# Whole-block normalisation and transposes, an even stride for the value rows, and a gate/up opening on 256 rows, in a fused attention and gated-MLP kernel

## The chip, the cores and the metric

The kernel runs on one core of one Trainium2 chip. The metric is device time in microseconds (us) from launch to end, the median of several executions. The profile of one execution gives a span 1.8 to 2.0 us shorter than the time measured for it. Where two kernels are compared, the numbers come from the same session on the same chip unless the text says otherwise.

## The reference, cut to what matters

```python
xn = layernorm(x)                                   # x: 2048 x 512, bf16
q  = (xn @ wq) -> 32 heads x 2048 x 128
p  = softmax(q @ k_cache^T * 128**-0.5)             # 2048 keys a head
s  = (p @ v_cache) -> 2048 x 4096, then @ wo        # 2048 x 512
g  = silu((relu(xn @ W_gate) * (xn @ W_up)) @ W_down)   # F = 1792
out = x + s * g
```

## The kernel before

The program first computes the gated MLP (160 us), then attention in 128 blocks. A block is one head and 512 query rows. It has 16 key tiles of 128 keys, taken in pairs. TensorE does, for each tile, one score matmul (512 columns) and four value matmuls (one for each 128 query rows, 129 columns: 128 values and a column of constants that sums the softmax denominator). ScalarE takes the exponential of a pair. The blocks are also the place where the query projection of the next head and the output projection of the last group of four heads (16 blocks) are done, one piece at the start of each block.

The value tile has rows of 129 elements, so 258 bytes:

```python
VW = Dh + 1                                          # 129
V_sb = [S_([128, KT, VW], BF16, "V_sb") for _ in range(2)]
...
def emit_PV_tile(gp, tt):
    ...
    for j in range(4):
        bank = j // 2
        if t == 0 and j % 2 == 0:
            _wait(pe, norm_tok[b - 1][bank] if b >= 1 else acc_free[bank])
        o_ap = ps_acc[:, bank, (j % 2) * 256:(j % 2) * 256 + VW]
        ins = pe.matmul(o_ap, PT[pb][:, tt, j * 128:(j + 1) * 128], V_sb[vb][:, t, :], ...)
```

At the end of a block, each of the two PSUM banks with its output is normalised by itself, and each 128 x 128 piece is transposed by its own DMA. The buffers for the normalised output number 16, one group, so VectorE waits at the first block of a group until every transpose of the group before has landed:

```python
NON = G * QB                                         # 16 buffers
def emit_norm_bank(b, bank, pvtok):
    _wait(dve, pvtok)
    if bank == 0 and b % (G * QB) == 0 and g >= 1:
        _wait(dve, t_tok(g - 1))
    rztok = dve.reciprocal(rz_sb[:, bank, :, :], z_ap)          # 128 x 2
    for jj in range(2):
        tok = dve.tensor_scalar(Onorm[ob][:, j, :], ps_acc[:, bank, base:base + Dh],
                                rz_sb[:, bank, jj, :], None, op0=ALU.mult)   # 128 x 128
    ...
    for jj in range(2):
        sp.dma_start_transpose(OT_store[...128 columns...], Onorm[ob][:, j, :])
```

The head of the program: 12 dummy matmuls to raise TensorE's clock, layer norm of the first four row tiles (two on GpSimd, two on VectorE), their transposes, and then gate and up on 512 rows for each 128 columns of the weights (`...` marks cuts):

```python
FCS = [0, min(2, FC), min(8, FC), FC]                # weights arrive in three parts
load_w(sp, Wg_sb, wg_src, sem_wg, 0)
load_w(act, Wu_sb, wu_src, sem_wu, 0)
...
for _i in range(12):
    pe.matmul(ps_acc[:, 0, 0:D], warm[:, 0:128], warm[:], start=True, stop=True)
head_ln()             # transposes of row tiles 0 to 3, then gate/up from the first column block on
```

The softmax here doesn't subtract the row's maximum and nothing guards it: scores larger than these inputs give would overflow.

Of the kernel before, what the change touches and what calls it, by code (L numbers as in the profile page):

```python
# [5 lines left out]
BF16 = mybir.dt.bfloat16  # L6
# [45 lines left out]
def bass_recurrent_scan__mha_block_cached__glu_gated_reglu__prompt_kernel(  # L52
# [33 lines left out]
    NON = G * QB  # L86
# [4 lines left out]
    TPG = 16 * 4 * G * QB  # L91
# [12 lines left out]
    with ExitStack() as es:  # L104
# [23 lines left out]
        V_sb = [S_([128, KT, VW], BF16, "V_sb") for _ in range(2)]  # L128
# [68 lines left out]
        with nc.Block() as block:  # L197

            @block.tensor
            def _(_pe_eng):  # L200
# [13 lines left out]
                FCS = [0, min(2, FC), min(8, FC), FC]  # L214
# [24 lines left out]
                load_w(act, Wu_sb, wu_src, sem_wu, 0)  # L239
# [103 lines left out]
                def head_transpose(n, ntok, eng, sem):  # L343
                    tp_ps = ps_r[:, n, :].bitcast(BF16)
# [13 lines left out]
                    ring_tok[n // 2].append(ctok)  # L358

                def head_ln():  # L360
                    st = ln_stats(0)
                    st = ln_stats(1)
                    sq01 = ln_aggr([0, 1], st)
                    st = ln_stats(2)
                    c01 = ln_coef([0, 1], sq01)
                    n0 = ln_norm(pool, sem_nm, 0, c01)
                    n1 = ln_norm(pool, sem_nm, 1, c01)
                    st = ln_stats(3)
                    sq23 = ln_aggr([2, 3], st)
                    c23 = ln_coef([2, 3], sq23)  # L370
                    n2 = ln_norm(dve, sem_ln4, 2, c23)
                    n3 = ln_norm(dve, sem_ln4, 3, c23)
                    head_transpose(0, n0, act, sem_xa)
                    head_transpose(1, n1, act, sem_xa)
                    head_transpose(2, n2, act, sem_xa)
                    head_transpose(3, n3, dve, sem_xt)

# [27 lines left out]

                def emit_gate_up(Q):
                    qs = slice(Q * NQ, (Q + 1) * NQ)
                    par = Q % 2
                    h_tok = None
                    for fc in range(FC):  # L410
                        fs = slice(fc * 128, (fc + 1) * 128)
                        s = ring_acquire()
# [16 lines left out]
                        gk = fc % NSLOT  # L429
                        _wait(act, gtok)  # L430
                        _wait(act, gr_free[gk])
                        rtok = sem_relu.sig(act.activation(gr_sb[gk][:], ps_r[:, gb, :], ACTF.Relu))  # L432
                        _wait(dve, gu_tok)
                        _wait(dve, rtok)
                        if fc == 0:
                            _wait(dve, hT_free[par])
                        h_tok = sem_h.sig(
                            dve.tensor_tensor(hT[par][:, fc, :], gr_sb[gk][:], ps_r[:, gb + 1, :], ALU.mult)  # L438
                        )
                        gr_free[gk] = h_tok  # L440
                        ring_tok[s] = [rtok, h_tok]
                        if Q == 0:
                            ln_task(fc)
# [33 lines left out]
                for _i in range(12):  # L477
                    pe.matmul(ps_acc[:, 0, 0:D], warm[:, 0:128], warm[:], start=True, stop=True)
                head_ln()
                ring_cnt[0] = 2  # L480
# [7 lines left out]
                rz_sb = S_([128, 2, 2, 1], F32, "rz_sb")  # L488
# [108 lines left out]
                def emit_norm_bank(b, bank, pvtok):  # L597
# [4 lines left out]
                    if bank == 0 and b % (G * QB) == 0 and g >= 1:  # L602
                        _wait(dve, t_tok(g - 1))
                    z_ap = ps_acc[:, bank, :].rearrange("p (j w) -> p j w", j=2)[:, :, Dh:Dh + 1]
                    rztok = sem_rz.sig(dve.reciprocal(rz_sb[:, bank, :, :], z_ap))  # L605
                    _wait(dve, rztok)
                    tok = None
                    for jj in range(2):
                        j = 2 * bank + jj
                        base = jj * 256  # L610
                        tok = sem_norm.sig(
                            dve.tensor_scalar(  # L612
                                Onorm[ob][:, j, :], ps_acc[:, bank, base:base + Dh],
                                rz_sb[:, bank, jj, :], None, op0=ALU.mult,
                            )
                        )
                    if b == NBLK - 1:
                        emit_last_transposes(hh, Q, ob, bank, tok)
                        return tok
                    _wait(sp, tok)  # L620
                    if bank == 0 and b % (G * QB) == 0 and g >= 2:
                        _wait(sp, opg_tok.get(g - 2))
                    tsem = sem_t[g % 2] if g < NG - 1 else sem_tl[Q]
                    for jj in range(2):
                        j = 2 * bank + jj
                        tsem.sig(
                            sp.dma_start_transpose(  # L627
                                OT_store[g % 2][:, hh, Q * NQ + j * 128:Q * NQ + (j + 1) * 128],
                                Onorm[ob][:, j, :],
                            )  # L630
                        )
# [26 lines left out]
                def emit_PV_tile(gp, tt):  # L658
# [11 lines left out]
                    for j in range(4):  # L670
# [4 lines left out]
                        ins = pe.matmul(o_ap, PT[pb][:, tt, j * 128:(j + 1) * 128], V_sb[vb][:, t, :],  # L675
                                        start=(t == 0 and j % 2 == 0), stop=(t == KT - 1 and j % 2 == 1))
                        if t == KT - 1 and j == 1:
# [3 lines left out]
                    if t == KT - 1:  # L681
# [3 lines left out]
                        ntx = emit_norm_bank(b, 0, tx)  # L685
                        nty = emit_norm_bank(b, 1, ty)
                        norm_tok[b] = (ntx, nty)
# [126 lines left out]
```

## Time and profile before

| | before |
|---|---|
| time, median of the first 3 runs | 1299.66 us (1298.06 to 1300.32) |
| span of the profile (of an execution that took 1300.44 us) | 1298.6 us |
| first value matmul starts at | 160.5 us |
| block period, blocks 1 to 15 / later | 8.254 / 8.835 us |
| gaps of TensorE after the first value matmul | 8.3 us |

The head of the page: busy time, share of the span, instructions. In all views PE is TensorE's matmuls, PEld its weight loads, DVE VectorE, ACT ScalarE, POOL GpSimd, and SPq the queue from which SyncE issues DMAs; L675 is line 675 of the kernel.

```profile
span 1298.6 us, 27683 instructions
...
PE 1287.6 (99%) x11968; PEld 835.3 (64%) x11968; DVE 442.5 (34%) x1190; ACT 1001.6 (77%) x1109; POOL 11.5 (1%) x23
...
## 4 chain that ended last, share of the span: by engine, by line
PE 93%; DVE 3%; SPq 2%; DMA 1%; issue 0%; ACT 0%; DVEq 0%
```

"PE 99% busy" says little, since a matmul's shown end overlaps the next one's start. The chain says more: 93% is TensorE's own work. What can be gained is in the other 7% and in TensorE's rate. The groups of the page for the value matmul and the normalisation (line, engine, operation, shapes, count | busy us, mean ns | idle before):

```profile
L675 PE MATMUL ps_acc<-V_sb,PT 128*128 128x129 bf16 x8192 | 784.2, 221 | 3.3 <-DVE Onorm L612 1.6
...
L605 DVE RECIPROCAL rz_sb<-ps_acc 128x2 f32<-128x2 f32 x256 | 42.3, 165 | 726.7 <-PE ps_acc L675 698.0
...
L612 DVE TENSOR_SCALAR Onorm<-ps_acc,rz_sb 128x128 bf16<-128x128 f32 x512 | 156.1, 347 | 9.2
```

The view of waits of before (engine, line waited for: us in total, times, longest us):

```profile
DVE rz_sb L605 <- PE ps_acc L675: 698.0, 123, 6.1
...
DVE rz_sb L605 <- DMA OT_store<-Onorm: 28.7, 4, 7.4
...
PEld ps_acc L675 <- DVE Onorm L612: 7.0, 21, 0.5
```

VectorE mostly waits for TensorE, as it should. TensorE waits for the normalisation 21 times. Four times VectorE waits for the transposes. The timeline of before at an ordinary block boundary in the first group (start us, duration, engine, line):

```profile
200.69 0.61 DVE L612 TENSOR_SCALAR Onorm<-ps_acc,rz_sb 128x128 bf16<-128x128 f32 x2
200.83 1.03 PE L515 MATMUL ps_r<-xnT,Wq_sb 128*128 128x512 bf16 x4
201.22 0.16 DVE L605 RECIPROCAL rz_sb<-ps_acc 128x2 f32<-128x2 f32 x1
...
201.42 0.61 DVE L612 TENSOR_SCALAR Onorm<-ps_acc,rz_sb 128x128 bf16<-128x128 f32 x2
201.70 0.91 PE L675 MATMUL ps_acc<-V_sb,PT 128*128 128x129 bf16 x8
```

The second half of the normalisation ends at 202.03. Two value matmuls of the next block have started from 201.70, and the third has to wait for that end: the eight take 0.91 us here. The timeline of before at the start of the second group:

```profile
299.22 0.39 PE L675 MATMUL ps_acc<-V_sb,PT 128*128 128x129 bf16 x4
...
300.86 0.17 DVE L605 RECIPROCAL rz_sb<-ps_acc 128x2 f32<-128x2 f32 x1 [7.44 <-DMA OT_store<-Onorm]
...
302.45 0.23 PE L675 MATMUL ps_acc<-V_sb,PT 128*128 128x129 bf16 x1 [0.36 <-DVE Onorm L612]
```

The bracket says that VectorE was idle for 7.44 us and that a transpose ended it. But the block's last value matmuls started only at 299.22. In an undisturbed block (last value matmuls 308.80, reciprocal 309.11) the normalisation follows after 0.31 us; here it follows after 1.64. So the transposes made it 1.3 us late, not 7.4: most of the idle time would have been there anyway.

The start-to-start distances of the matmuls, worked out from the starts in the trace (mean ns to the next matmul's start, gaps above 70 ns left out for value matmuls):

```
before                      even key tiles   odd key tiles
value matmul                     56.72            57.36
score matmul ahead of it        216.67           215.80
```

### The profile page before, as it was taken

What the parts mean: (1) busy time and instruction counts of PE and PEld (TensorE: products, weight loads), DVE (VectorE), ACT (ScalarE), POOL (GpSimd) and SP (SyncE); (2) the same over time, 40 slices, a digit from 0 to 9 for tenths busy, and PEclk for the clock granted to TensorE, in tenths of its full rate; (3) what the DMA queues carried; (4) which work ended last, traced back from release to release, by engine and by line L of the source; (5) the groups of instructions that cost most, each with busy time, mean ns of one, the idle gap of its engine ahead of it and who ended that gap; (6) DMA issues with size and microseconds to landing.
All of it is one profiled execution on the core that took longest, in us unless ns stands there. A gap on an engine that the chain in (4) does not pass through costs nothing.

```text
span 1298.6 us, 27683 instructions
## 1 busy us (share of the span) xinstructions
PE 1287.6 (99%) x11968; PEld 835.3 (64%) x11968; DVE 442.5 (34%) x1190; ACT 1001.6 (77%) x1109; POOL 11.5 (1%) x23
## 2 busy tenths in 40 slices
PE   9999999999999999999999999999999999999998
PEld 4444466666666666666666666666666666666665
DVE  6333322222323323323323323323323322334456
ACT  3322399888888888888888888888888888888884
POOL 2000000000000000000000000000000000000000
PEclk9999999999999999999999999999999999999999
DMA  9500112222222322232211322232223211232202
GB/s 259 114 1 1 21 39 47 47 56 42 52 52 54 68 52 54 52 68 53 53 36 34 69 52 54 52 69 54 52 52 53 69 36 33 52 68 54 47 16 73
DMA packets 250999, 71.69 MB, mean 55 GB/s; under 512 B 237824, under 2 KB 250880, under 8 KB 250880
## 3 DMA queue, kind: packets, MB, share of 16 engines
q1 hardware_dynamic: 250064, 69.41, 25.2%
q8 instruction: 95, 1.56, 0.5%
q10 hardware_dynamic: 816, 0.52, 0.1%
q14 instruction: 24, 0.20, 0.1%
HBM read 32.77 MB, written 2.10 MB: 27 GB/s over the span
## 4 chain that ended last, share of the span: by engine, by line
PE 93%; DVE 3%; SPq 2%; DMA 1%; issue 0%; ACT 0%; DVEq 0%
PE ps_acc L675 35%; PE ps_r L582 32%; PE ps_r L515 7%; PE ps_r L536 7%; PE ps_r L422 4%; PE ps_acc L459 4%; PE ps_r L426 4%; DVE Onorm L612 2%; SPq L627 2%; PE ps_r L709 1%; DMA OT_store<-Onorm 1%; DVE rz_sb L605 0%; DMA x_sb<-in_A_x_dram 0%; DVE stats L313 0%; DVE s_acc L561 0%
## 5 line engine op out<-in xcount | busy, mean ns | idle before, releaser
L592 ACT ACTIVATE PT<-ps_r 128x1024 bf16<-128x1024 f32 x1024 | 952.5, 1050 | 179.0 <-PE ps_r L582 179.0
L675 PE MATMUL ps_acc<-V_sb,PT 128*128 128x129 bf16 x8192 | 784.2, 221 | 3.3 <-DVE Onorm L612 1.6
L675 PEld LDWEIGHTS ps_acc<-V_sb,PT 128*128 128x128 bf16 x8192 | 623.1, 98 | 249.3 <-DVE Onorm L612 7.0
L582 PE MATMUL ps_r<-QT_sb,KT_sb 128*128 128x512 bf16 x2048 | 755.1, 380 | 0.0
L605 DVE RECIPROCAL rz_sb<-ps_acc 128x2 f32<-128x2 f32 x256 | 42.3, 165 | 726.7 <-PE ps_acc L675 698.0
L582 PEld LDWEIGHTS ps_r<-QT_sb,KT_sb 128*128 128x128 bf16 x2048 | 195.4, 98 | 1.1 <-DVE QT_sb L526 0.4
L612 DVE TENSOR_SCALAR Onorm<-ps_acc,rz_sb 128x128 bf16<-128x128 f32 x512 | 156.1, 347 | 9.2
L515 PE MATMUL ps_r<-xnT,Wq_sb 128*128 128x512 bf16 x512 | 130.9, 379 | 0.0
L536 PE MATMUL ps_r<-Wo_sb,OT_store 128*128 128x512 bf16 x448 | 114.7, 379 | 0.0
L515 PEld LDWEIGHTS ps_r<-xnT,Wq_sb 128*128 128x128 bf16 x512 | 49.8, 97 | 60.8 <-ACT PT L592 24.2
L526 DVE CAST QT_sb<-ps_r 128x512 bf16<-128x512 f32 x128 | 87.2, 681 | 0.7 <-PE ps_r L515 0.7
L536 PEld LDWEIGHTS ps_r<-Wo_sb,OT_store 128*128 128x128 bf16 x448 | 43.6, 98 | 53.4 <-DMA OT_store<-Onorm 1.2
L432 ACT ACTIVATE gr_sb<-ps_r 128x512 bf16<-128x512 f32 x56 | 33.4, 597 | 54.2 <-PE ps_r L422 54.0
L549 DVE TENSOR_TENSOR s_acc<-s_acc,ps_r 128x512 f32<-128x512 f32 x96 | 66.0, 687 | 13.3 <-PE ps_r L536 1.1
L422 PE MATMUL ps_r<-xnT,Wg_sb 128*128 128x512 bf16 x224 | 57.5, 379 | 0.6 <-DVE xnT L356 0.6
L426 PE MATMUL ps_r<-xnT,Wu_sb 128*128 128x512 bf16 x224 | 57.5, 379 | 0.0
L438 DVE TENSOR_TENSOR hT<-gr_sb,ps_r 128x512 bf16<-128x512 bf16 x56 | 38.4, 687 | 47.2 <-PE ps_r L426 44.4
L459 PE MATMUL ps_acc<-Wd_sb,hT 128*128 128x512 bf16 x224 | 49.0, 379 | 0.0
L465 ACT ACTIVATE sig_sb<-ps_acc 128x512 f32<-128x512 f32 x16 | 9.6, 597 | 38.8 <-PE ps_acc L459 38.8
L422 PEld LDWEIGHTS ps_r<-xnT,Wg_sb 128*128 128x128 bf16 x224 | 21.8, 98 | 26.9 <-ACT xnT L356 0.7
L459 PEld LDWEIGHTS ps_acc<-Wd_sb,hT 128*128 128x128 bf16 x224 | 21.9, 98 | 26.4
L426 PEld LDWEIGHTS ps_r<-xnT,Wu_sb 128*128 128x128 bf16 x224 | 21.9, 98 | 26.4
(36 smaller groups left out, 126.4 us busy)
## 6 DMA issues: line engine op xcount, KB each, us to landing
V_sb<-in_A_v_cache_dram SPq DMA_DIRECT2D x32, 512.0 KB, 5.3
OT_store<-Onorm SPq DMA_TRANSPOSE x508, 2.4
Wq_sb<-in_A_wq_dram SPq DMA_DIRECT2D x32, 128.0 KB, 2.8
Wo_sb<-in_A_wo_dram SPq DMA_DIRECT2D x8, 512.0 KB, 4.2
Wd_sb<-in_B_W_down_dram SPq DMA_DIRECT2D x1, 1792.0 KB, 13.5
Wg_sb<-in_B_W_gate_dram SPq DMA_DIRECT2D x2, 768.0 KB, 9.7
Wu_sb<-in_B_W_up_dram SPq DMA_DIRECT2D x2, 768.0 KB, 10.4
x_sb<-in_A_x_dram SPq DMA_DIRECT2D x3, 512.0 KB, 10.8
```

Source lines behind the costliest of these rows:

```text
L422: ins = pe.matmul(ps_r[:, gb, :], Wg_sb[:, c, fs], xnT[:, c, qs], start=(c == 0), stop=(c == DC - 1))
L426: ins = pe.matmul(ps_r[:, gb + 1, :], Wu_sb[:, c, fs], xnT[:, c, qs], start=(c == 0), stop=(c == DC - 1))
L459: ins = pe.matmul(ps_acc[:, jb, 0:D], hT[par][:, fc, j * 128:(j + 1) * 128], Wd_sb[:, fc, :], start=(fc == 0), stop=(fc == FC - 1))
L515: ins = pe.matmul(ps_r[:, bank, :], Wq_sb[b][:, c, :], xnT[:, c, qs], start=(c == 0), stop=(c == DC - 1))
L526: etok = sem_qpe.sig(dve.tensor_copy(QT_sb[b][:, qs], ps_r[:, bank, :]))
L536: ins = pe.matmul(ps_r[:, bank, 0:D], OT_store[g % 2][:, hh, n * 128:(n + 1) * 128], Wo_sb[g % 2][:, hh, :], start=(hh == 0), stop=(hh == ...
L549: dve.tensor_tensor(s_acc[:, n, :], s_acc[:, n, :], ps_r[:, bank, 0:D], ALU.add)
L582: ins = pe.matmul(ps_r[:, 2 * s + tt, :], KT_sb[h % 2][:, t * 128:(t + 1) * 128], QT_sb[h % 2][:, qs], start=True, stop=True)
L592: act.activation(PT[pb][:], ps_r[:, 2 * s:2 * s + 2, :], ACTF.Exp, scale=scale)
L605: rztok = sem_rz.sig(dve.reciprocal(rz_sb[:, bank, :, :], z_ap))
L612: dve.tensor_scalar(Onorm[ob][:, j, :], ps_acc[:, bank, base:base + Dh], rz_sb[:, bank, jj, :], None, op0=ALU.mult,)
L675: ins = pe.matmul(o_ap, PT[pb][:, tt, j * 128:(j + 1) * 128], V_sb[vb][:, t, :], start=(t == 0 and j % 2 == 0), stop=(t == KT - 1 and j % ...
```

## The change

Its intent: normalise a block in one reciprocal and one multiply, and transpose it in one DMA, so that TensorE no longer waits for VectorE and fewer DMAs are issued; give the group four more buffers and move the wait for the old group four blocks in; give value rows an even number of bytes between them that is a multiple of 4 (272); open gate and up on the first 256 rows while the other rows are still being normalised.

```diff
-    NON = G * QB
+    NON = G * QB + 4
+    VS = Dh + 8
-    TPG = 16 * 4 * G * QB
+    TPG = 16 * G * QB
-        V_sb = [S_([128, KT, VW], BF16, "V_sb") for _ in range(2)]
+        V_sb = [S_([128, KT, VS], BF16, "V_sb") for _ in range(2)]
...
-                FCS = [0, min(2, FC), min(8, FC), FC]
+                FCS = [0, min(3, FC), min(8, FC), FC]
+                HFC = 3
-                load_w(act, Wu_sb, wu_src, sem_wu, 0)
+                load_w(sp, Wu_sb, wu_src, sem_wu, 0)
...
-                    n0 = ln_norm(pool, sem_nm, 0, c01)
-                    n1 = ln_norm(pool, sem_nm, 1, c01)
+                    n0 = ln_norm(dve, sem_ln4, 0, c01)
+                    n1 = ln_norm(dve, sem_ln4, 1, c01)
+                    head_transpose(0, n0, act, sem_xa)
+                    head_transpose(1, n1, act, sem_xa)
+                    warm_mm(3)
...
+                    emit_half(0, range(HFC - 1), xt_ready[0][0:2])   # 256-row gate and up
...
+                    emit_half(0, range(HFC - 1, HFC), [])
+                    emit_half(1, range(HFC), xt_ready[0][2:4])
...
-                def emit_norm_bank(b, bank, pvtok):
+                def emit_norm_block(b, pvtok):
-                    if bank == 0 and b % (G * QB) == 0 and g >= 1:
+                    if b % (G * QB) == 4 and g >= 1:
                         _wait(dve, t_tok(g - 1))
...
+                    rtok = sem_rz.sig(dve.reciprocal(rz_sb[:], z_ap))            # 128 x 4
+                    tok = sem_norm.sig(
+                        dve.tensor_tensor(Onorm[ob][:], o_ap, rz_sb[:].to_broadcast([128, 4, Dh]), ALU.mult))
...
+                        sp.dma_start_transpose(
+                            OT_store[g % 2][:, hh, Q * NQ:(Q + 1) * NQ].rearrange("p (j q) -> p j q", j=4),
+                            Onorm[ob][:].rearrange("p j d -> p (j d)")))
...
-                        ins = pe.matmul(o_ap, PT[pb][:, tt, j * 128:(j + 1) * 128], V_sb[vb][:, t, :],
+                        ins = pe.matmul(o_ap, PT[pb][:, tt, j * 128:(j + 1) * 128], V_sb[vb][:, t, 0:VW],
```

The last block keeps a normalisation in two halves, each now one reciprocal and one multiply of 256 columns.

More of the change, by code (lines that the diff above doesn't have):

```diff
@@ L343, in head_transpose @@
                 def head_transpose(n, ntok, eng, sem):
-                    tp_ps = ps_r[:, n, :].bitcast(BF16)
+                    tp_ps = acc_bf[n % 2]
+                    _wait(pe, acc_free[n % 2])
                     if n == 0:
@@ L357, in head_transpose, with warm_mm @@
                     xt_ready[0].append(ctok)
-                    ring_tok[n // 2].append(ctok)
+                    acc_free[n % 2] = ctok
+                def warm_mm(k):
+                    for _i in range(k):
+                        pe.matmul(ps_r[:, 2 * NSLOT - 1, 0:D], warm[:, 0:128], warm[:], start=True, stop=True)
                 def head_ln():
@@ L372, in head_ln, with emit_half @@
                     n3 = ln_norm(dve, sem_ln4, 3, c23)
-                    head_transpose(0, n0, act, sem_xa)
-                    head_transpose(1, n1, act, sem_xa)
                     head_transpose(2, n2, act, sem_xa)
                     head_transpose(3, n3, dve, sem_xt)
+                    emit_half(0, range(HFC - 1, HFC), [])
+                    emit_half(1, range(HFC), xt_ready[0][2:4])
+                half_slots = []
+                def emit_half(k, fcs, toks):
+                    hs = slice(k * 256, (k + 1) * 256)
+                    for fc in fcs:
+                        fs = slice(fc * 128, (fc + 1) * 128)
+                        if k == 0:
+                            if fc == 0:
+                                pe.wait_ge(sem_wg[0].h, 16)
+                            half_slots.append(ring_acquire())
+                        if fc == 0:
+                            _wait_all(pe, toks)
+                        s = half_slots[fc]
+                        for i, W in enumerate((Wg_sb, Wu_sb)):
+                            if k == 0 and fc == 0 and i == 1:
+                                pe.wait_ge(sem_wu[0].h, 16)
+                            ins = None
+                            for c in range(DC):
+                                ins = pe.matmul(ps_r[:, 2 * s + i, hs], W[:, c, fs], xnT[:, c, hs],
+                                                start=(c == 0), stop=(c == DC - 1))
+                            if k == 1:
+                                half_tok[(fc, i)] = (sem_gate if i == 0 else sem_gu).sig(ins)
+                half_tok = {}
                 ln_hold = {}
@@ L404, in _, with finish_gate_up @@
                 hT_free = [None, None]
+                def finish_gate_up(Q, fc, s, gtok, gu_tok):
+                    par = Q % 2
+                    gb = 2 * s
+                    gk = fc % NSLOT
+                    _wait(act, gtok)
+                    _wait(act, gr_free[gk])
+                    rtok = sem_relu.sig(act.activation(gr_sb[gk][:], ps_r[:, gb, :], ACTF.Relu))
+                    _wait(dve, gu_tok)
+                    _wait(dve, rtok)
+                    if fc == 0:
+                        _wait(dve, hT_free[par])
+                    h_tok = sem_h.sig(
+                        dve.tensor_tensor(hT[par][:, fc, :], gr_sb[gk][:], ps_r[:, gb + 1, :], ALU.mult)
+                    )
+                    gr_free[gk] = h_tok
+                    ring_tok[s] = [rtok, h_tok]
+                    if Q == 0:
+                        ln_task(fc)
+                    return h_tok
                 def emit_gate_up(Q):
                     qs = slice(Q * NQ, (Q + 1) * NQ)
-                    par = Q % 2
                     h_tok = None
@@ L411, in emit_gate_up @@
                         fs = slice(fc * 128, (fc + 1) * 128)
+                        if Q == 0 and fc < HFC:
+                            s = half_slots[fc]
+                            finish_gate_up(Q, fc, s, half_tok[(fc, 0)], half_tok[(fc, 1)])
+                            continue
                         s = ring_acquire()
@@ L428, in emit_gate_up @@
                         gu_tok = sem_gu.sig(ins)
-                        gk = fc % NSLOT
-                        _wait(act, gtok)
-                        _wait(act, gr_free[gk])
-                        rtok = sem_relu.sig(act.activation(gr_sb[gk][:], ps_r[:, gb, :], ACTF.Relu))
-                        _wait(dve, gu_tok)
-                        _wait(dve, rtok)
-                        if fc == 0:
-                            _wait(dve, hT_free[par])
-                        h_tok = sem_h.sig(
-                            dve.tensor_tensor(hT[par][:, fc, :], gr_sb[gk][:], ps_r[:, gb + 1, :], ALU.mult)
-                        )
-                        gr_free[gk] = h_tok
-                        ring_tok[s] = [rtok, h_tok]
-                        if Q == 0:
-                            ln_task(fc)
+                        h_tok = finish_gate_up(Q, fc, s, gtok, gu_tok)
                     return h_tok
@@ L476, in _ @@
                 _wait(pe, warm_w)
-                for _i in range(12):
-                    pe.matmul(ps_acc[:, 0, 0:D], warm[:, 0:128], warm[:], start=True, stop=True)
+                warm_mm(12)
                 head_ln()
-                ring_cnt[0] = 2
                 for Q in range(QB):
@@ L487, in _ @@
                 s_acc = S_([128, NT, D], F32, "s_acc")
-                rz_sb = S_([128, 2, 2, 1], F32, "rz_sb")
+                rz_sb = S_([128, 4, 1], F32, "rz_sb")
                 Onorm = [S_([128, 4, Dh], BF16, "Onorm") for _ in range(NON)]
@@ L595, in emit_S_tile, with acc_view @@
                     ring_tok[s] = [etok]
-                def emit_norm_bank(b, bank, pvtok):
+                def acc_view():
+                    v = ps_acc[:].rearrange("p k (j w) -> p (k j) w", j=2)
+                    return v[:, :, 0:Dh], v[:, :, Dh:Dh + 1]
+                def emit_norm_block(b, pvtok):
                     h, Q = divmod(b, QB)
@@ L601, in emit_norm_bank @@
                     _wait(dve, pvtok)
-                    if bank == 0 and b % (G * QB) == 0 and g >= 1:
+                    if b % (G * QB) == 4 and g >= 1:
                         _wait(dve, t_tok(g - 1))
-                    z_ap = ps_acc[:, bank, :].rearrange("p (j w) -> p j w", j=2)[:, :, Dh:Dh + 1]
-                    rztok = sem_rz.sig(dve.reciprocal(rz_sb[:, bank, :, :], z_ap))
-                    _wait(dve, rztok)
-                    tok = None
-                    for jj in range(2):
-                        j = 2 * bank + jj
-                        base = jj * 256
-                        tok = sem_norm.sig(
-                            dve.tensor_scalar(
-                                Onorm[ob][:, j, :], ps_acc[:, bank, base:base + Dh],
-                                rz_sb[:, bank, jj, :], None, op0=ALU.mult,
-                            )
-                        )
@@ L617, in emit_norm_bank @@
-                    if b == NBLK - 1:
-                        emit_last_transposes(hh, Q, ob, bank, tok)
-                        return tok
+                    o_ap, z_ap = acc_view()
+                    rtok = sem_rz.sig(dve.reciprocal(rz_sb[:], z_ap))
+                    _wait(dve, rtok)
+                    tok = sem_norm.sig(
+                        dve.tensor_tensor(Onorm[ob][:], o_ap, rz_sb[:].to_broadcast([128, 4, Dh]), ALU.mult))
                     _wait(sp, tok)
-                    if bank == 0 and b % (G * QB) == 0 and g >= 2:
+                    if b % (G * QB) == 0 and g >= 2:
@@ L622, in emit_norm_bank @@
                         _wait(sp, opg_tok.get(g - 2))
                     tsem = sem_t[g % 2] if g < NG - 1 else sem_tl[Q]
-                    for jj in range(2):
-                        j = 2 * bank + jj
-                        tsem.sig(
-                            sp.dma_start_transpose(
-                                OT_store[g % 2][:, hh, Q * NQ + j * 128:Q * NQ + (j + 1) * 128],
-                                Onorm[ob][:, j, :],
-                            )
-                        )
+                    tsem.sig(
+                        sp.dma_start_transpose(
+                            OT_store[g % 2][:, hh, Q * NQ:(Q + 1) * NQ].rearrange("p (j q) -> p j q", j=4),
+                            Onorm[ob][:].rearrange("p j d -> p (j d)")))
@@ new lines, in emit_norm_block, with emit_norm_last @@
+                    return tok
+                def emit_norm_last(b, bank, pvtok):
+                    h, Q = divmod(b, QB)
+                    g, hh = divmod(h, G)
+                    ob = b % NON
+                    _wait(dve, pvtok)
+                    o_ap, z_ap = acc_view()
+                    js = slice(2 * bank, 2 * bank + 2)
+                    rtok = sem_rz.sig(dve.reciprocal(rz_sb[:, js, :], z_ap[:, js, :]))
+                    _wait(dve, rtok)
+                    tok = sem_norm.sig(
+                        dve.tensor_tensor(Onorm[ob][:, js, :], o_ap[:, js, :],
+                                          rz_sb[:, js, :].to_broadcast([128, 2, Dh]), ALU.mult))
+                    emit_last_transposes(hh, Q, ob, bank, tok)
@@ L674, in emit_PV_tile @@
                         o_ap = ps_acc[:, bank, (j % 2) * 256:(j % 2) * 256 + VW]
-                        ins = pe.matmul(o_ap, PT[pb][:, tt, j * 128:(j + 1) * 128], V_sb[vb][:, t, :],
+                        ins = pe.matmul(o_ap, PT[pb][:, tt, j * 128:(j + 1) * 128], V_sb[vb][:, t, 0:VW],
                                         start=(t == 0 and j % 2 == 0), stop=(t == KT - 1 and j % 2 == 1))
-                        if t == KT - 1 and j == 1:
+                        if b == NBLK - 1 and t == KT - 1 and j == 1:
                             tx = sem_pv.sig(ins)
@@ L684, in emit_PV_tile @@
                             issue_v(h + 2)
-                        ntx = emit_norm_bank(b, 0, tx)
-                        nty = emit_norm_bank(b, 1, ty)
-                        norm_tok[b] = (ntx, nty)
+                        if b < NBLK - 1:
+                            ntok = emit_norm_block(b, ty)
+                            norm_tok[b] = (ntok, ntok)
+                        else:
+                            emit_norm_last(b, 0, tx)
+                            emit_norm_last(b, 1, ty)
                 def sp_head_start(h):
```

## The prediction

> **What bounds it.** TensorE: by the chain of waits 93% of the 1298.6 us span is its work. In attention its matmuls (timeline) start without a gap: a 512-column matmul every 216 ns, a 129-column value matmul every 57 ns. A block (16 score, 64 value, 4 query, 4 output matmuls) takes 24x216 + 64x57 = 8.83 us; the trace's block period is 8.835. ScalarE (8 exponentials at 0.91 us a block) and VectorE (34% busy) have room. Only TensorE's rate and gaps can pay. Its gaps after the first value matmul add up to only 8.3 us:
> - blocks 1 to 16 (no output projection yet): 0.27 us each before the third value matmul, 4.3 us in all. They wait for the second half of the previous block's normalisation (two reciprocals at 165 ns, four scalings at 347 ns, issued 0.26 us apart), covered by only six 512-column matmuls (1.30 us).
> - group starts (blocks 17, 49, 65, 113): 2.5 us. VectorE sat up to 7.4 us (28.7 us in four waits, by the view of waits) until the last group's output transposes had landed; the DMA queue issues four a block at 1.2 to 2.6 us each.
> - the last head 0.65 us, the final transposes 0.6.
>
> **The change, costed.**
> 1. Whole-block normalisation: one reciprocal (165 ns) and one 512-element multiply from PSUM. The s_acc addition of that size took 687 ns, so expect that (the Trainium skill, "VectorE: DVE Perf Modes", "Why PSUM operands drop a tier": fp32 from PSUM stays at one element per cycle; 687 ns agrees). It ends some 1.15 us after the last value matmul starts, where TensorE has 1.35 us of other work. Those waits vanish: -4.3 us. VectorE's 90 us less busy time is worth nothing by itself.
> 2. One transpose a block instead of four, four more buffers, and the wait four blocks later: VectorE's 28.7 us of waits vanish; TensorE gains 2.5, with some of the last head's: -2.9 us.
> 3. Even stride. With 129-element rows odd key tiles start on a 2-byte, even ones on a 4-byte boundary. Value matmul starts are 57.30 ns apart in odd tiles, 56.67 in even ones (the Trainium skill, "TensorE: Matmul & The Clock Gate", "Back-to-back issue gap": N/2.4 + 2.5, 56.25 for 129; the trace is slightly above). 4096 matmuls x 0.63 ns, all critical: -2.6 us.
> 4. Opening on 256 rows: the first gate matmul moves from 9.36 us to about 8.0, but halves cost slightly more, and the second half waits behind the first and two copies. The first three column blocks should end at 13.8 us instead of 14.54: -0.6 us, uncertain (the up weights now queue behind the gate weights).
>
> Sum: -4.3 -2.9 -2.6 -0.6 = -10.4 us. **Predicted 1289.3 us, 8 in 10 between 1286.8 and 1293.0.** Faster by over 2%: 1%; within: 98%; slower: 1%.
>
> **What would show it.** (1) Block period of the first group 7.95 us, not 8.25; no value matmul waits for the normalisation. (2) No wait of VectorE for output transposes. (3) Odd and even tiles both 56.7 ns apart; later block period 8.81. (4) First value matmul near 159.9 us instead of 160.5.
>
> **What would make it wrong.** A multiply above 0.85 us would bring back waits in the first group (margin 0.15 to 0.2 us). The odd-tile cost may not be alignment. Without the waits the exponentials or the ring of three score slots may hold TensorE instead. Late weights may leave the head no gain.

## The result, and the profile after

| | before | after |
|---|---|---|
| time, median of 4 runs each | 1299.99 us (1298.06 to 1300.76) | 1287.97 us (1287.70 to 1288.06) |
| span of the profile | 1298.6 | 1285.8 |
| first value matmul starts at | 160.5 | 159.5 |
| block period, blocks 1 to 15 / later | 8.254 / 8.835 | 7.943 / 8.807 |
| gaps of TensorE after the first value matmul | 8.3 | 0.9 |

The ratio is 0.9909, with a 95% interval of 0.9892 to 0.9927. Note the spread as well: 2.7 us before, 0.4 us after.

The page of after:

```profile
span 1285.8 us, 26847 instructions
...
PE 1279.2 (99%) x11995; PEld 834.8 (65%) x11995; DVE 380.0 (30%) x682; ACT 1001.4 (78%) x1109; POOL 10.0 (1%) x21
...
## 4 chain that ended last, share of the span: by engine, by line
PE 99%; DVE 1%; issue 0%; DMA 0%; ACT 0%
...
L722 PE MATMUL ps_acc<-V_sb,PT 128*128 128x129 bf16 x8192 | 776.5, 220 | 0.0
...
L652 DVE RECIPROCAL rz_sb<-ps_acc 128x4 f32<-128x4 f32 x127 | 23.3, 183 | 729.6 <-PE ps_acc L722 729.6
...
L655 DVE TENSOR_TENSOR Onorm<-ps_acc,rz_sb 128x512 bf16<-128x512 f32 x127 | 87.8, 691 | 4.4
```

The chain is now 99% TensorE. The value matmul has no idle time before it. The multiply takes 691 ns (predicted 687) and the reciprocal 183 (165). The only line of the view of waits that names the normalisation's first instruction in ordinary blocks is this one; the wait for the transposes is not there:

```profile
DVE rz_sb L652 <- PE ps_acc L722: 729.6, 126, 6.1
```

The timeline of after at the boundary that was shown of before:

```profile
198.28 0.18 DVE L652 RECIPROCAL rz_sb<-ps_acc 128x4 f32<-128x4 f32 x1 [5.96 <-PE ps_acc L722]
198.50 0.69 DVE L655 TENSOR_TENSOR Onorm<-ps_acc,rz_sb 128x512 bf16<-128x512 f32 x1
198.51 1.03 PE L558 MATMUL ps_r<-xnT,Wq_sb 128*128 128x512 bf16 x4
199.22 1.19 SPq L661 DMA_TRANSPOSE OT_store<-Onorm  x1
199.37 0.62 PE L722 MATMUL ps_acc<-V_sb,PT 128*128 128x129 bf16 x8
```

The multiply ends at 199.19, 0.18 us before TensorE comes to the next value matmuls at 199.37, and the eight take 0.62 us. That is the margin the prediction gave (0.15 to 0.2 us).

The start-to-start distances in the trace of after, worked out as above:

```
after                       even key tiles   odd key tiles
value matmul                     56.67            56.67
score matmul ahead of it        215.83           215.83
```

Where the 12.8 us between the two spans went, from the two traces: the first value matmul is 1.05 us earlier; the gaps shrank by 7.4 us (4.3 in blocks 1 to 16, 2.6 at group starts, 0.5 in the last head); the distances of the matmuls shrank by 3.7 us; the tail after the last value matmul went from 12.21 to 11.84 us. That is 12.5 us; 0.3 us are rounding and what the cutoffs leave out.

### The profile page after: what moved, and what is told of

Read it like the earlier page. It is cut to its first block, busy times and chain, and to the rows that moved or that the text cites. A ratio compares the mean times of both kernels' runs of the same rounds, so it can differ in the third digit from the quotient of the medians.

```text
span 1285.8 us, 26847 instructions
## 1 busy us (share of the span) xinstructions
PE 1279.2 (99%) x11995; PEld 834.8 (65%) x11995; DVE 380.0 (30%) x682; ACT 1001.4 (78%) x1109; POOL 10.0 (1%) x21
## 4 chain that ended last, share of the span: by engine, by line
PE 99%; DVE 1%; issue 0%; DMA 0%; ACT 0%
PE ps_acc L722 36%; PE ps_r L625 34%; PE ps_r L558 9%; PE ps_r L579 8%; PE ps_acc L504 4%; PE ps_r L485 4%; PE ps_r L481 4%; PE ps_r L759 1%; DVE fin_tmp L767 0%; PE ps_r L407 0%; DMA x_sb<-in_A_x_dram 0%; DVE stats L315 0%; ACT xnT L359 0%; PE ps_acc L353 0%; DVE x_sb L772 0%
## 5 line engine op out<-in xcount | busy, mean ns | idle before, releaser
L652 DVE RECIPROCAL rz_sb<-ps_acc 128x4 f32<-128x4 f32 x127 | 23.3, 183 | 729.6 <-PE ps_acc L722 729.6
L655 DVE TENSOR_TENSOR Onorm<-ps_acc,rz_sb 128x512 bf16<-128x512 f32 x127 | 87.8, 691 | 4.4
L485 PE MATMUL ps_r<-xnT,Wu_sb 128*128 128x512 bf16 x212 | 54.4, 379 | 0.0
L481 PE MATMUL ps_r<-xnT,Wg_sb 128*128 128x512 bf16 x212 | 54.4, 379 | 0.0
```

Of the source, the lines that this page charges most:

```text
L481: ins = pe.matmul(ps_r[:, gb, :], Wg_sb[:, c, fs], xnT[:, c, qs], start=(c == 0), stop=(c == DC - 1))
L485: ins = pe.matmul(ps_r[:, gb + 1, :], Wu_sb[:, c, fs], xnT[:, c, qs], start=(c == 0), stop=(c == DC - 1))
L655: dve.tensor_tensor(Onorm[ob][:], o_ap, rz_sb[:].to_broadcast([128, 4, Dh]), ALU.mult))
```

## The experiments

For every run the trace gives three numbers that separate the parts: the start of the first gate matmul, the time from the first to the last value matmul, and the gaps in it. They are worked out from the starts of TensorE's matmuls. In the traces of before_again, after_no_warm, stride_130 and after_split_norm, about 230 of some 12000 matmul records are missing, nearly all of score matmuls; no value matmul is, so the three numbers stand.

| run | first gate matmul, us | gate to first value matmul | first to last value matmul | time, median us |
|---|---|---|---|---|
| before (first trace) | 9.36 | 151.18 | 1125.88 | 1299.99 |
| before_again | 9.56 | 152.57 | 1124.06 | 1298.68 |
| stride_only | 9.11 | 151.18 | 1120.44 | 1294.75 |
| norm_only | 9.23 | 151.18 | 1119.47 | 1294.69 |
| one_transpose_and_wait | 9.19 | 151.18 | 1123.10 | 1298.14 |
| head_only | 8.17 | 151.69 | 1123.62 | 1296.79 |
| after | 7.80 | 151.68 | 1114.51 | 1287.97 |
| all_odd | 8.47 | 151.68 | 1121.30 | 1294.92 |
| after_four_transposes | 8.57 | 151.68 | 1114.58 | 1288.22 |
| after_old_wait | 8.13 | 151.68 | 1114.50 | 1287.94 |
| after_old_head | 9.17 | 152.76 | 1114.50 | 1289.41 |
| after_no_warm | 8.02 | 151.68 | 1114.51 | 1288.63 |
| stride_130 | 8.26 | 151.69 | 1114.73 | 1288.33 |
| after_split_norm | 8.19 | 151.68 | 1119.46 | 1293.04 |

All kernels gave correct results. Four of them (before_again, after_no_warm, stride_130, after_split_norm) ran on one chip, on which before took 1298.52 us in the same session; the other experiments ran on another, on which it took 1298.85 to 1298.97. The time of after is that of its own, first session.

### The stride alone (stride_only)

```diff
 # on the kernel before
+    VS = Dh + 8
-        V_sb = [S_([128, KT, VW], BF16, "V_sb") for _ in range(2)]
+        V_sb = [S_([128, KT, VS], BF16, "V_sb") for _ in range(2)]
-                        ... V_sb[vb][:, t, :],
+                        ... V_sb[vb][:, t, 0:VW],
```

> Only the row stride of the value tile changes (129 to 136 elements); normalisation, transposes and head as before. Theory (a value row on a 2-byte boundary slows its own four matmuls and the one after): odd and even tiles both start every 56.67 ns, score matmuls every 215.8 ns instead of 216.7 before even tiles; the span falls by about 3.9 us, 1299.7 to about 1295.8, ratio 0.997. The sum in the prediction (own four matmuls alone) would say 2.6 us. Rival (the odd-tile spacing comes from the normalisation and transpose traffic, which the change also thinned out): odd tiles stay at 57.3 ns and the time stays at about 1299.7.

Measured: 1294.75 us against 1298.85, ratio 0.9966 (0.9953 to 0.998). Odd tiles came to 56.66 ns, and score matmuls to 215.82 and 215.83. The time from first to last value matmul fell by 5.44 us, of which 1.88 us are smaller gaps, nearly all at the group starts of this one trace (6.40 us of gaps in all, against 8.28); the remaining 3.56 us are the stride. The rival falls: nothing else was changed and the odd tiles changed at once.

### Every row on a 2-byte boundary (all_odd)

```diff
 # on the kernel after: the rows still 136 elements apart, each one element later
-                        ... V_sb[vb][:, t, 0:VW],
+                        ... V_sb[vb][:, t, 1:1 + VW],
-    pool.memset(V_sb[b][:, :, Dh:VW], 2.0)
+    pool.memset(V_sb[b][:, :, 1 + Dh:1 + VW], 2.0)
-    sp.dma_start(V_sb[b][:, :, 0:Dh], src)
+    sp.dma_start(V_sb[b][:, :, 1:1 + Dh], src)
```

> The kernel after, its value rows still 136 elements apart but each starting one element later, so that every row of every tile starts on a 2-byte boundary (before, every second tile did). Theory (the boundary of the moving rows sets the spacing): all 16 tiles at 57.3 ns, the score matmuls between them slowed by up to 0.85 ns each, twice the cost of before: 1288.0 + 2 x 3.9 = about 1295.5, between 1294 and 1296. Rival 1 (it is the row stride of 258 bytes, not the start): spacing stays 56.67 ns and the time 1288. Rival 2 (only the alternation of odd and even costs): less than 3.9 us more.

Measured: 1294.92 us, first to last value matmul 6.79 us longer than in after. All tiles stood at 57.30 and 57.32 ns and all score matmuls between value matmuls at 216.65 to 216.66. So the cost follows the start of the rows, not the stride, and doubling the number of such tiles doubles it: 3.40 us for half of them, beside 3.56 in the run above.

### A stride of 130 (stride_130)

```diff
 # on the kernel after
-    VS = Dh + 8
+    VS = Dh + 2
```

> The kernel after with value rows 130 elements apart instead of 136: every row starts on a 4-byte boundary, few on an 8- or 16-byte one. Theory (only the 4-byte boundary matters, since before, even tiles at 4 and at 8 bytes had the same 56.67 ns): spacing 56.67 ns everywhere, 1288.0 us. Rival (a 16-byte boundary is needed): some tiles slower, up to 1295.

Measured: 1288.33 us; value matmuls 56.65 ns apart in even tiles and 56.74 in odd ones, score matmuls 215.85. A 4-byte boundary removes the cost seen before; the 0.09 ns in odd tiles would be worth 0.4 us, and the time from first to last value matmul is 0.22 us longer than in after. That small rest is not explained. The 16-byte rival falls.

### The normalisation alone (norm_only)

```diff
 # on the kernel before; four transposes, 16 buffers and the wait at the group start stay
-                        ntx = emit_norm_bank(b, 0, tx)
-                        nty = emit_norm_bank(b, 1, ty)
+                        ntok = emit_norm_block(b, ty)      # one reciprocal, one multiply of 512 columns
```

> Only the whole-block normalisation; four transposes a block, 16 buffers and the wait at the group start stay, rows stay at 129. Theory (the first-group waits come from the end of the two half normalisations): block period of the first group 7.97 us instead of 8.25, no wait before the third value matmul there, -4.3 us; at the group starts VectorE still waits for the transposes, but TensorE's stall shrinks from 0.7 to about 0.2 us because the normalisation after it is 0.4 to 0.5 us shorter, -1.5 us; with the last head's 0.4 about -6 us in all, 1299.7 to about 1293.7. Rival (starting the normalisation later, after the last value matmul, costs what the shorter work gains): a wait now before the first value matmul of each block, gain under 2 us.

Measured: 1294.69 us against 1298.85, ratio 0.9963 (0.9951 to 0.9976), so about -4.2 us. The waits in blocks 1 to 16 were gone, with a block period of 7.972 us. One thing was not foreseen: at block 17 TensorE stood still for 1.3 us ahead of the first output projection, which needed the group's last transposes. In the trace the four issues of those transposes took 7.15 us, behind the key transpose and the value load of the next heads. VectorE still waited for the transposes:

```profile
DVE rz_blk L610 <- DMA OT_store<-Onorm: 27.8, 4, 8.2
```

Yet apart from block 17 TensorE lost only 0.02 us at the group starts of this trace: at block 48 the normalisation began 0.9 us late both here and in stride_only, and TensorE then lost 0.02 us here and 0.34 there. So the shorter normalisation by itself takes up much of a late landing. First to last value matmul, the two traces differ by 6.41 us, near the 6 expected; the timed runs gain less, and part of that is that the first trace of before had lost more at its group starts than most runs do (see before_again).

### The normalisation undone in after (after_split_norm)

```diff
 # on the kernel after; one transpose, late wait, even stride and new head stay
-                            ntok = emit_norm_block(b, ty)
-                            norm_tok[b] = (ntok, ntok)
+                            norm_tok[b] = (emit_norm_split(b, 0, tx), emit_norm_split(b, 1, ty))
```

> The kernel after with the normalisation in two halves again (two reciprocals, four scalings of 128 columns); one transpose a block, even stride and new head stay. Theory: the waits before the third value matmul of blocks 1 to 16 come back, about 0.28 us each, 4.5 us, and 0.4 to 0.5 us in the last head: 1292.5 to 1293.0. Rival (they came from VectorE being held up by something else that the change took away): no wait, 1288.0.

Measured: 1293.04 us, first to last value matmul 4.95 us longer than in after. The block period of the first group went back to 8.225 us, 0.282 more than in after. The line of the view of waits came back with nearly the counts of before:

```profile
PEld ps_acc L755 <- DVE Onorm L682: 5.0, 17, 0.5
```

This is the largest part of the change, and it is shown from both sides.

### The transposes and the late wait alone (one_transpose_and_wait)

```diff
 # on the kernel before; normalisation still in two halves
-    NON = G * QB
+    NON = G * QB + 4
-                    if bank == 0 and b % (G * QB) == 0 and g >= 1:
+                    if bank == 0 and b % (G * QB) == 4 and g >= 1:
+                    if bank == 0:
+                        return tok
-                    for jj in range(2): ... dma_start_transpose(128 columns)
+                    ... one dma_start_transpose(512 columns)
```

> Only the transposes: one a block instead of four, 20 buffers, the wait four blocks into the group; the normalisation stays in two halves, rows at 129. Theory (group-start stalls come from VectorE waiting for the landing of the last transposes): no wait of VectorE for output transposes, no stall at blocks 17, 49, 65, 113, the 0.27 us waits of blocks 1 to 16 stay: about -2.5 us, 1299.7 to about 1297.2. Rival (the stalls come from the two-half normalisation at all block boundaries): no change.

Measured: 1298.14 us against 1298.85, ratio 0.999 (0.9977 to 1.0002). In the trace the stalls at the group starts are all gone, the wait of VectorE for the transposes is gone, and the 0.27 us waits of blocks 1 to 16 stay. Mechanism right, size wrong: a typical run of before loses less at the group starts than the first trace showed. The kernel before, traced again, says why.

### The kernel before again (before_again)

```diff
 # no edit
```

> The kernel before once more, for a second trace and for the spread. Theory (before has two things that vary from run to run: the landing of the last transposes at four to seven group starts, 0.3 to 2.5 us together, and a chance that the TensorE clock falls to half at the start of gate and up, 1.7 us, as the trace of the kernel after with the old head shows): runs spread over 1298 to 1301 us, the stalls at the group starts of this trace differ from the 2.5 us of the first one by over 0.5 us, while the 16 waits of 0.27 us come back to within 0.02 us each. Rival (the group-start stalls are fixed): 2.5 us again at blocks 17, 49, 65, 113.

Measured: 1298.68 us (1298.39 to 1300.37). The stalls at the group starts came at blocks 17, 49 and 113 and added up to 0.95 us, not 2.6 (the traces of stride_only and head_only, which have the same transposes and the same wait, show 1.0 and 0.5); the waits of blocks 1 to 16 were the same to 0.01 us. The group-start loss depends on when the last transpose happens to land and varies from run to run; one trace is not a measure of it. This trace also caught the second thing that varies: a slow start of gate and up, taken up below.

### Four transposes again, and the old wait again (after_four_transposes, after_old_wait)

```diff
 # after_four_transposes, on the kernel after
-    TPG = 16 * G * QB
+    TPG = 16 * 4 * G * QB
-                    tsem.sig(... one dma_start_transpose(512 columns))
+                    for j in range(4):
+                        tsem.sig(... dma_start_transpose(128 columns))
 # after_old_wait, on the kernel after
-    NON = G * QB + 4
+    NON = G * QB
-                    if b % (G * QB) == 4 and g >= 1:
+                    if b % (G * QB) == 0 and g >= 1:
```

> The kernel after with four output transposes a block again; buffers and the late wait stay. Theory (with the wait moved, a transpose only has to land within a block): VectorE has no wait for them; but at block 17 the first output projection needs the whole first group, and with the shorter blocks four issues behind the key transpose and the value load come late, as in the run of the normalisation alone, where TensorE stood still 1.3 us there: +0.3 to +1.5 us at that block, nothing elsewhere, 1288.3 to 1289.5, with more spread between runs than after has. Rival (issues do not matter): 1288.0, no stall.

> The kernel after with 16 buffers and VectorE's wait back at the first block of a group; one transpose a block stays. Theory (the wait at the boundary is the cause, whatever the number of issues): VectorE waits again at some group starts for the last block's transpose, issue 1.6 us and landing 2.4 to 3.2 us behind the key and value loads, 3 to 7 us a time; behind each wait the normalisation runs late and TensorE loses 0.1 to 0.3 us (up to seven times): 1288.3 to 1289.5. Rival (fewer issues alone cured it): no wait over 2 us, no stall, 1288.0.

Measured: 1288.22 and 1287.94 us, against 1287.97 of after in its own session; first to last value matmul 1114.58 and 1114.50, as in after (1114.51). Neither trace has a wait of VectorE for the transposes, and TensorE has no stall at a group start. I had expected a stall from each, and both expectations failed. So each of the two parts removes VectorE's wait by itself: with one transpose a block the landing comes early enough for the old wait, and with the late wait four transposes do no harm. Together they do not pay twice. What either is worth to TensorE with a normalisation in two halves these two runs do not show, since both keep the whole-block one, which in norm_only already took up much of a late landing. Why four transposes stalled the first output projection in norm_only and not here is not settled; it is one trace of each, and the landing varies.

### The head alone, and the head undone (head_only, after_old_head)

```diff
 # head_only: the text from the weight loads to the end of the MLP taken from after, the rest from before
 # after_old_head: the same text taken from before, the rest from after
```

> Only the head: gate and up opened on 256 rows, three column blocks, first weights on one queue, first four row tiles normalised on VectorE. Theory: the first value matmul moves from 160.5 to about 159.5 us, -1.06 us, of which about 0.4 us because the x tiles land earlier when the up weights do not share the second queue. Sum in the prediction: -0.6 us. Rival (the earlier start in the profile of after was chance between runs): no change outside the noise of about 1 us.

> The kernel after with the head of before (512 rows, two column blocks, up weights on the second queue, first two row tiles normalised on GpSimd). Theory: first value matmul back from 159.5 to 160.4 us, nothing else, +0.6 to +1.0 us, 1288.7 to 1289.0, measured more cleanly than in the run of the head alone, because here no group-start stall varies. Rival (that run's 2 us gain is real, the head also helps something later): +2 us, about 1290.

Measured: head_only 1296.79 us against 1298.85, ratio 0.9981 (0.9968 to 0.9993). after_old_head 1289.41 us: 1288.65, 1288.77, 1290.05 and 1290.22, two groups 1.4 us apart. That head_only gained 2.1 us where 0.6 or 1.06 were expected does not measure the opening, because the time of before also holds the varying group starts and the slow starts told of here. The trace of after_old_head fell on a slow run and shows what the groups are. The view of windows (us, busy time of each engine, then the granted clock of TensorE) of after_old_head:

```profile
6.00:9.00 3.00, 1.61 (x17) 0.92 (x16) 2.04 (x8) 1.95 (x4) 1.38 (x2) 1.00 1.00 343
9.00:12.50 3.50, 3.33 (x9) 1.22 (x10) 0.07 (x1) 0.60 (x1) 0.00 (x0) 0.51 1.07 380
```

The same stretch in head_only, in before and in before_again, in this order:

```profile
9.00:12.50 3.50, 3.50 (x38) 3.19 (x37) 0.81 (x3) 1.18 (x2) 0.00 (x0) 1.00 1.08 363
9.00:12.50 3.50, 3.14 (x15) 1.50 (x16) 0.94 (x2) 1.08 (x3) 0.00 (x0) 1.00 1.08 375
9.00:12.50 3.50, 2.94 (x8) 1.08 (x9) 0.19 (x1) 0.66 (x2) 0.00 (x0) 0.51 1.07 371
```

In after_old_head the clock was 0.51 from 9.0 to 12.5 us; in before, with the same head, it was full. The timeline of after_old_head shows gate and up at half speed (four 512-column matmuls in 1.86 us):

```profile
9.17 1.86 PE L423 MATMUL ps_r<-xnT,Wg_sb 128*128 128x512 bf16 x4 [0.56 <-DVE xnT L357]
10.83 1.82 PE L427 MATMUL ps_r<-xnT,Wu_sb 128*128 128x512 bf16 x4
```

Gate to first value matmul took 152.76 us there instead of 151.18: 1.6 us lost. before_again shows the same (clock 0.51 in that stretch, 152.57). In six traces with the old head it happened twice; in eight with the new head never. The timed runs agree: in each of the eight kernels with the new head (34 runs) the spans lie within 1.0 us of one another, while two of the four runs of after_old_head have spans 1.5 to 1.7 us longer than the other two. That the clock falls after TensorE has been idle is what the Trainium skill states ("TensorE: Matmul & The Clock Gate", "What's actually happening": half clock is the state after an idle window of about 3.4 us, and the window runs freely, so its phase varies). The half clock agrees: start-to-start was 427 ns in these matmuls, which is the page's cold figure for 512 columns (426.7 ns, "Wait — 56ns, not 53.3ns?"). The idle window itself is not seen here: between the last dummy matmul (until about 6.1 us) and the first gate matmul (9.17) TensorE did sixteen transposes. Nor does the length of that stretch decide: it was 3.1 and 3.5 us in the two traces whose clock fell, and 3.3 to 3.6 us in the four that kept it. What differs in the record of the clock is when it first rose: at 5.59 us in both traces where it fell, then half clock from 9.00 and full again from 12.42, in steps of 3.41 us; at 4.67 to 5.43 us in the four where it stayed. That fits a window of fixed length whose place decides, but no run tries it.

Without such a run, the head's gain is small and steady. The first gate matmul starts at 9.27 us in the mean of the six traces with the old head and at 8.20 in the mean of the eight with the new one; gate to first value matmul then takes 0.50 us more, because 256-column matmuls start 109 ns apart, more than half of 216, and the second half is interrupted by transposes. Net 0.57 us. The 1.05 us between the traces of before and after was partly luck: 7.80 us was the earliest of the eight.

### Without the three dummy matmuls (after_no_warm)

```diff
 # on the kernel after
-                    warm_mm(3)
```

> The kernel after without the three dummy matmuls between the first transposes and the first gate matmul. Theory (they keep the clock up; an idle TensorE there lets it fall in some runs): in one to three of five runs about 1.7 us more, so a spread of over 1 us where after has 0.4; the other runs at 1288.0. Rival (the earlier opening alone keeps the clock up): all five within 0.5 us of 1288.0, gate matmuls at full clock.

Measured: 1288.63 us, 1288.00 to 1288.93, full clock in the trace. Four of the five times lie over 0.5 us above 1288.0, as the rival did not foresee, but that is not in the kernel's work: the spans of all five are 1285.9 to 1286.0 us, as in after (1285.8 to 1286.2), and four of the times exceed their span by 2.7 to 3.0 us where the fifth exceeds it by 2.0. So there is no slow start among five, my theory falls and the rival stands: in this sample the earlier opening alone is enough (about 2.0 us without ordinary matmuls, from 6.0 to 8.02, in place of 3.1 to 3.6 with the old head). That the new head prevents the fall is supported by the counts (2 of 6 against 0 of 8 traces, and the spans above); why it does is argued, not proven.

## Why the prediction was right

The prediction, 1289.3 us (1286.8 to 1293.0), was right: 1287.97 us, 1.3 us below its centre. That the sum fits is partly luck. Against the later medians of before the gain is 10.6 to 11.0 us, near the forecast 10.4, but there the group starts and the last head give 1.5 us less than forecast (0.95 + 0.4 in before_again, in place of 2.9), the odd tiles about 1.0 more, and the tail 0.4 that was not forecast. Point by point:

- **Bound by TensorE; ScalarE and the ring of score slots (the three PSUM buffers that the score matmuls fill in turn) do not take over.** Right. The chain went from 93% to 99% TensorE, and the gaps from 8.3 to 0.9 us. The block period of 7.943 and 8.807 us answers to the forecast of 7.95 and 8.81.
- **First-group waits, -4.3 us.** Right: -4.3 us in the trace of after; +4.95 us, of which 0.45 belong to the last head, when the normalisation was undone.
- **Group starts and last head, -2.9 us.** Mechanism right. Against the first trace of before it was -3.1 us. But against a typical run it is less: 0.95 us at the group starts in the second trace of before, and the run of this part alone gained 0.7 us, with an interval that holds zero. The step at fault is the reading of 2.5 us as a fixed cost from one trace.
- **Odd tiles, -2.6 us.** Mechanism right, the term too small: 3.4 to 3.6 us. Two numbers were off. The value matmuls of odd tiles lost 0.69 ns each, not 0.63 (in the forecast, the mean of the middle tiles). And the matmul that follows an odd tile, a score matmul, starts its own successor 0.85 ns late, about 0.85 us in all over some thousand of them. It is the term "4096 matmuls x 0.63 ns" that was mis-sized: it counted the slow instruction and not what it hands on.
- **Opening on 256 rows, -0.6 us.** Right in the mean (0.57 us). What it did not see is the clock: the old head falls to half clock for 3.4 us in some runs and then loses 1.4 to 1.6 us. That, with the varying group starts, can explain why before spreads over 2.7 us and after over 0.4, and why the two medians differ by more in the session of the prediction (12.0 us) than against before's later medians (10.6 to 11.0).
- **The tail, no gain forecast.** From the last value matmul to the end it takes 11.82 to 11.84 us in after and the seven kernels made from it, and 12.19 to 12.21 us in the six traces of kernels made from before. The eight, and only they, have the last block's normalisation of after (two multiplies of 256 columns, 424 ns each, in place of four of 347). No other part of the change moved it (12.19 to 12.21 us in stride_only, norm_only, one_transpose_and_wait and head_only). That this is the cause is argued, not tried alone.

No version in these runs beats after: after_old_wait equals it (1287.94), and the remaining gaps of TensorE after the first value matmul are 0.9 us.

## What to carry to other kernels

When one engine runs without gaps, compare the start-to-start times of its instructions across tiles that should be alike: a difference of 0.7 ns between odd and even rows, with the 0.85 ns it handed on to the matmul after them, was worth some 3.5 us here, and the cure was seven unused elements a row. A wait that the profile puts at 7.4 us may be 1.3 us of lateness, so subtract what the engine would have waited anyway, and look at a second trace before taking a landing time for a constant. Two parts of a change that cure the same wait do not add up, and only undoing one at a time shows it.

## What the Trainium skill lacked or had wrong

- "SBUF — State Buffer", "Operand start alignment": says that bf16 operands may start 2 bytes past a 4-byte boundary and that this is about legality, its runs having timed nothing. The runs add the speed for TensorE's moving operand: 129-column matmuls start 57.3 ns apart on a 2-byte boundary and 56.67 on a 4-byte one, and the score matmul after such a tile starts its successor 0.82 to 0.85 ns late (before, all_odd, stride_130).
- "TensorE: Matmul & The Clock Gate", "Back-to-back issue gap": N/2.4 + 2.5 gives 56.25 ns for 129 columns; 56.67 was measured. The same section's figure for a stream of 512-column matmuls with weight loads, about 131 ns each, is not what was seen here: 216 ns, its isolated figure.
- "TensorE: Matmul & The Clock Gate", "Why this matters for your kernels": it warns of idle gaps above about 3 us between matmul bursts. In after_old_head the clock fell (0.51) though from the last dummy matmul to the first gate matmul its longest idle stretch was 0.7 us; counted without the sixteen transposes it was 3.1 us. The page's "PE-mode transpose" says that transposes do not count as busy in the same way, which would fit; no run here tries it. But the same stretch without the transposes was 3.3 to 3.6 us in four traces that kept full clock (before, stride_only, norm_only, one_transpose_and_wait), so a length alone does not foretell the fall.
- No page has the cost of one DMA transpose of 128 x 512 from SBUF to SBUF against four of 128 x 128: 1.19 us to issue and 2.4 us to land, against four times 1.23 us to issue and 2.4 us to land (medians).
